# Hash-bucket attention: the bucket mask as sign bits, with its bias in the exponential's scale

## The chip, the cores and the metric

The kernel runs on one core of a Trainium2 chip. The metric is the device time of one execution in microseconds (us). The core has a matrix engine (PE, with its weight loads shown apart as PEld), a vector engine (DVE), a scalar engine for activations (ACT), a general engine (POOL), and a queue engine (SP) that issues DMAs. Each engine works through its own list in order; ACT and POOL also issue DMAs.

## What is computed

Two stages run in one kernel. The first is attention over 4 x 8 heads of 768 tokens with head size 64, where a query sees a key only if both fall into the same hash bucket. The bucket is made of six bits, each the sign of a projection:

```python
q_bits = (np.einsum('bhsd,dk->bhsk', q, proj) > 0).astype(np.int64)
k_bits = (np.einsum('bhsd,dk->bhsk', k, proj) > 0).astype(np.int64)
q_bucket = np.sum(q_bits * powers, axis=-1)      # powers of two
...
mask = q_bucket[:, :, :, None] == k_bucket[:, :, None, :]
scores = scale * np.matmul(q, k.transpose(0, 1, 3, 2))
scores = np.where(mask, scores, -1000000000.0)
...
attn = np.exp(scores)
attn = attn / (np.sum(attn, axis=-1, keepdims=True) + 1e-09)
return np.matmul(attn, v).astype(np.float32)
```

The second stage takes the 3072 x 512 result through an RMS norm and a gated feed-forward layer (`silu(xn @ w_gate) * (xn @ w_val) @ w_out`, inner size 1536).

## The kernel before

All heads are worked one after the other, i = 0 to 31, and the prologue of a head runs two heads ahead of its main part (the loop at L379 to L389). A planner orders each engine's instructions and sets the waits; the source does not write that order out.

**Prologue of a head (L136 to L249).** For q and then for k, a DMA on SP's queue loads the head (L145). PE transposes it in six blocks (L153) into PSUM, in two halves of 384 tokens. DVE copies each half to the float32 tile `tf` (L157) and casts it to bf16 into rows 0 to 63 of `tq` (L159, times the softmax scale) or `tk` (L167). PE multiplies `tf` by the projection (L171), which leaves six rows of 384 numbers in PSUM. DVE compares them with zero and writes rows 64 to 69 of the same tile: 0 or 120 for a query (L179), -0.5 or +0.5 for a key (L188). These six rows make the score matmul add a term that depends on the bits in common. Next comes a bias per key: six matmuls with one output column each (L214) multiply the key's six bit rows by -60, and DVE adds -178 (L221). With it the exponent is the score plus 2 where all bits agree, and lower by at least 60 where one differs. Last, a row for a small term of the denominator is made (L234, L243).

All PSUM tiles of the prologue (transposes, projections, biases, the small row, and the sums of the RMS norm) take turns in one pool, `pro`, that has two buffers. A third tile must wait until the first has been read.

**Main part of a head (L251 to L330).** For each of six key blocks, PE makes 128 x 768 scores (L269, 70 rows deep) in one of two score buffers, and ACT takes the exponential to fp16 with the per-key bias (L278). PE accumulates values times exponentials (L289, L298). DVE moves the result to SBUF (L308); the denominator goes to DRAM and back on POOL's queue, DVE inverts it (L317), and it returns as a broadcast (L322) for the multiplication into `xt` (L325).

**RMS norm (L332 to L377).** For each 512 tokens ACT squares (L337), PE sums (L338), ACT takes a square root (L351), and DVE inverts one row of 512 (L355) and corrects it (L357 to L364). The row goes through DRAM to a broadcast, and POOL multiplies (L375). Four of the six blocks run within the attention loop, when the last head of their batch is done.

**Weights.** ACT's queue issues 20 loads of feed-forward weights, one emitted with each of the first 20 heads (L122, L133). They use one or two staging buffers, which DVE empties by a cast (L123, L134).

**Feed-forward (L391 to L440).** Six blocks of 512 tokens: 96 matmuls for gate and value (L403, L411), a sigmoid on ACT (L419), two DVE products (L421, L424), then the output matmuls (L429).

Of the kernel before, what the change touches and what calls it, by code (L numbers as in the profile page):

```python
# [9 lines left out]
FP32 = mybir.dt.float32  # L10
BF16 = mybir.dt.bfloat16
FP16 = mybir.dt.float16

AF = mybir.ActivationFunctionType
ALU = mybir.AluOpType
# [3 lines left out]
def kernel(  # L19
# [12 lines left out]
    nc = tc.nc  # L32

    B, H, S, D = q.shape
    NB = S // 128
# [7 lines left out]
    NTS = NT // 512  # L43
    scale = 1.0 / (D ** 0.5)

    QSCL = 120.0
    KOFF = 0.5
    BETA = 2.0
    BIAS_RHS = -60.0
    BIAS_ADD = BETA - 180.0  # L50
    DELTA = 1.0e-9

    def ts_ready_head(tsi):
# [4 lines left out]
    const = ctx.enter_context(tc.tile_pool(name="const", bufs=1))  # L58
# [7 lines left out]
    nc.gpsimd.memset(proj_sb[:], 0.0)  # L66
    nc.scalar.dma_start(out=proj_sb[0:64, 0:n_bits], in_=proj[:, :])

    biascol = const.tile([128, 1], BF16, tag="c_biascol")
    nc.gpsimd.memset(biascol[:], BIAS_RHS)  # L70
    deltacol = const.tile([128, 1], FP16, tag="c_deltacol")
    nc.gpsimd.memset(deltacol[:], 1.0)
    ones_bf = const.tile([128, 512], BF16, tag="c_onesbf")
# [6 lines left out]
    for dc in range(NDC):  # L80
        nc.scalar.dma_start(
            out=rmsg_col[0:128, dc : dc + 1],
            in_=moe_rms_g[bass.ts(dc, 128)].rearrange("(p x) -> p x", x=1),
# [16 lines left out]
    bias_sb_tiles = [None] * NHEAD  # L100
# [8 lines left out]
    with (  # L109
# [26 lines left out]
        def emit_prologue(i):  # L136
            b, h = head_bh(i)
            tq = att.tile([128, S], BF16, name=f"tq{i}", tag="tqk", bufs=8)
            tk = att.tile([128, S], BF16, name=f"tk{i}", tag="tqk", bufs=8)
            tq_tiles[i] = tq  # L140
            tk_tiles[i] = tk

            for which, src, tdst in (("q", q, tq), ("k", k, tk)):
                nat = att.tile([128, NB, 64], FP32, tag="qknat", bufs=6)
                nc.sync.dma_start(  # L145
                    out=nat[:], in_=src[b, h].rearrange("(p n) d -> p n d", n=NB)
                )
                tf = att.tile([64, S], FP32, tag="tf", bufs=3)
                for half in range(2):
                    tps = pro_ps.tile([64, 3, 128], FP32, tag="pro")  # L150
                    for j in range(3):
                        sc = half * 3 + j
                        nc.tensor.transpose(  # L153
                            out=tps[:, j, :], in_=nat[:, sc, :], identity=ident[:]
                        )
                    cols = bass.ds(half * 384, 384)
                    nc.vector.tensor_copy(out=tf[0:64, cols], in_=tps[:, :, :])  # L157
                    if which == "q":
                        nc.vector.tensor_scalar(  # L159
                            out=tdst[0:64, cols],  # L160
                            in0=tf[0:64, cols],
                            scalar1=scale,
                            scalar2=None,
                            op0=ALU.mult,
                        )
                    else:
                        nc.vector.tensor_copy(out=tdst[0:64, cols], in_=tf[0:64, cols])  # L167
                for half, n in ((0, 384), (1, 384)):
                    bps = pro_ps.tile([128, n], FP32, tag="pro")
                    cols = bass.ds(half * 384, n)  # L170
                    nc.tensor.matmul(  # L171
                        out=bps[64:70, 0:n],
                        lhsT=proj_sb[0:64, 0:n_bits],
                        rhs=tf[0:64, cols],
                        start=True,
                        stop=True,
                    )
                    if which == "q":
                        nc.vector.tensor_scalar(  # L179
                            out=tdst[64:70, cols],  # L180
                            in0=bps[64:70, 0:n],
                            scalar1=0.0,
                            scalar2=QSCL,
                            op0=ALU.is_gt,
                            op1=ALU.mult,
                        )
                    else:
                        nc.vector.tensor_scalar(  # L188
                            out=tdst[64:70, cols],
                            in0=bps[64:70, 0:n],  # L190
                            scalar1=0.0,
                            scalar2=KOFF,
                            op0=ALU.is_gt,
                            op1=ALU.subtract,
                        )

            if h % 2 == 0:
                vt = att.tile([128, NB, 193], FP16, name=f"vt{i}", tag="vt", bufs=3)
                vt_tiles[i // 2] = vt
                nc.gpsimd.memset(vt[:, :, 64:66], 1.0)  # L200
                nc.gpsimd.memset(vt[:, :, 66:129], 0.0)
                for hh, col0 in ((h, 0), (h + 1, 129)):
                    vnat = att.tile([128, NB, 64], FP32, tag="vnat", bufs=2)
                    nc.sync.dma_start(
                        out=vnat[:],
                        in_=v[b, hh].rearrange("(p n) e -> p n e", n=NB),
                    )
                    nc.vector.tensor_copy(out=vt[:, :, col0 : col0 + 64], in_=vnat[:])

            bias_sb = att.tile([128, 8], FP32, name=f"bias{i}", tag="bsb", bufs=4)  # L210
            bias_sb_tiles[i] = bias_sb
            bps = pro_ps.tile([128, 8], FP32, tag="pro")
            for kc in range(NB):
                nc.tensor.matmul(  # L214
                    out=bps[0:128, kc : kc + 1],
                    lhsT=tk[64:70, bass.ts(kc, 128)],
                    rhs=biascol[64:70, 0:1],
                    start=True,
                    stop=True,
                )  # L220
            nc.vector.tensor_scalar(  # L221
                out=bias_sb[0:128, 0:NB],
                in0=bps[0:128, 0:NB],
                scalar1=BIAS_ADD,
                scalar2=None,
                op0=ALU.add,
            )

            vcols = bass.ds(0, 65) if h % 2 == 0 else bass.ds(65, 128)
            M = 65 if h % 2 == 0 else 128  # L230
            vt = vt_tiles[i // 2]
            vbps = pro_ps.tile([1, 128], FP32, tag="pro")
            for jc in range(NB):
                nc.tensor.matmul(  # L234
                    out=vbps[0:1, 0:M],
                    lhsT=deltacol[0:128, 0:1],
                    rhs=vt[:, jc, vcols],
                    start=(jc == 0),
                    stop=(jc == NB - 1),
                )  # L240
            vbrow = att.tile([1, 128], BF16, name=f"vbr{i}", tag="vbr", bufs=4)
            vbrow_tiles[i] = vbrow
            nc.vector.tensor_scalar(  # L243
                out=vbrow[0:1, 0:M],
                in0=vbps[0:1, 0:M],
                scalar1=DELTA / float(S),
                scalar2=None,
                op0=ALU.mult,
            )  # L249

        def emit_main(i):  # L251
# [1 line left out]
            even = h % 2 == 0  # L253
            tq = tq_tiles[i]
            tk = tk_tiles[i]
            bias_sb = bias_sb_tiles[i]
            vt = vt_tiles[i // 2]
            vbrow = vbrow_tiles[i]
            dci = h // 2
# [6 lines left out]
            for kc in range(NB):  # L266
                sct = sc_ps.tile([128, 1024], FP32, tag="sc")
                for qs, n in ((0, 512), (1, 256)):
                    nc.tensor.matmul(  # L269
                        out=sct[0:128, bass.ds(qs * 512, n)],  # L270
                        lhsT=tk[0:70, bass.ts(kc, 128)],
                        rhs=tq[0:70, bass.ds(qs * 512, n)],
                        start=True,
                        stop=True,
                    )
                u = att.tile([128, S], FP16, name=f"u{i}_{kc}", tag="u", bufs=6)
                u_tiles[i][kc] = u
                nc.scalar.activation(  # L278
                    out=u[:, :],
                    in_=sct[0:128, 0:S],  # L280
                    func=AF.Exp,
                    bias=bias_sb[0:128, kc : kc + 1],
                    scale=1.0,
                )

            avt = av_ps.tile([128, 1024], FP32, name=f"av{i}", tag="av")
            for jc in range(NB):
                for qs, n in ((0, 512), (1, 256)):
                    nc.tensor.matmul(  # L289
                        out=avt[0:M, bass.ds(qs * 512, n)],  # L290
                        lhsT=vt[:, jc, vcols],
                        rhs=u_tiles[i][jc][:, bass.ds(qs * 512, n)],
                        start=(jc == 0),
                        stop=False,
                    )
                u_tiles[i][jc] = None
            for qs, n in ((0, 512), (1, 256)):
                nc.tensor.matmul(  # L298
                    out=avt[0:M, bass.ds(qs * 512, n)],
                    lhsT=vbrow[0:1, 0:M],  # L300
                    rhs=ones_bf[0:1, 0:n],
                    start=False,
                    stop=True,
# [167 lines left out]
```

## Time and profile before

| quantity | value |
|---|---|
| median of 6 runs | 666.25 us (641.85 to 676.97) |
| the profiled execution: its time, and the span of its instructions | 640.58 us, 638.8 us |
| PE busy | 569.9 us (89%) |
| DVE busy | 424.0 us (66%) |
| ACT busy | 244.3 us (38%) |
| POOL busy | 110.3 us (17%) |
| mean granted PE clock | 0.909 |

The profile is of one execution. Its page gives busy time by engine, then the span in 40 slices of 16 us with the clock granted to PE in tenths of full speed, then groups of instructions by source line (count, busy time, mean length in ns, and the idle time before them with what ended it). A busy PE is not a PE at its peak, because matmuls overlap and their ends are modelled; so the distance from one start to the next tells more than a length. Rows of a timeline give start, length, engine, line, operation, and in brackets the idle time before and what ended it.

### The profile page before, as it was taken

The numbers are of one execution on the slowest core, as the hardware profiler recorded it, in microseconds if no ns is written. First come the engines' busy times: TensorE is split into PE (matmuls) and PEld (weight loads), VectorE is DVE, ScalarE is ACT, GpSimd is POOL, SyncE is SP. The second block draws the span as 40 slices with busy tenths as digits, with TensorE's granted clock in tenths as the row PEclk, the third lists the DMA queues.
The fourth block names the chain that finished last, engine by engine and source line by source line (L and its number), as shares of the span: only waits on it lengthen the run. The fifth ranks groups of instructions, "written<-read, shape, count | busy, mean of one in ns | idle before, by whom it ended". The sixth has DMA issues, their size and how long they took to land. (4 is left out here: it accounts for less than half of the span.)

```text
span 638.8 us, 7718 instructions
## 1 busy us (share of the span) xinstructions
PE 569.9 (89%) x2744; PEld 234.2 (37%) x2744; DVE 424.0 (66%) x794; ACT 244.3 (38%) x312; POOL 110.3 (17%) x196
## 2 busy tenths in 40 slices
PE   1999999979999956999997899984998999999997
PEld 0334343423443311334342233331443434444443
DVE  2668678786777768658778656532839395748473
ACT  0245454443645461445554235332333241313130
POOL 1002212223212224322131302112003020000000
PEclk9999899986999975889997769657999999999999
DMA  8536544432234331232331111001010101010101
GB/s 257 181 114 197 168 131 114 116 116 62 68 88 112 88 87 47 62 88 79 97 108 48 41 46 51 25 27 51 1 66 18 66 18 50 17 63 4 67 1 66
DMA packets 27362, 49.57 MB, mean 78 GB/s; under 512 B 6582, under 2 KB 18870, under 8 KB 27324
## 3 DMA queue, kind: packets, MB, share of 16 engines
q1 hardware_dynamic: 18156, 26.76, 13.4%
q0 software_dynamic: 5632, 12.89, 7.4%
q10 hardware_dynamic: 3536, 9.44, 4.5%
q8 instruction: 21, 0.34, 0.2%
q14 instruction: 17, 0.14, 0.1%
HBM read 42.57 MB, written 6.50 MB: 77 GB/s over the span
## 5 line engine op out<-in xcount | busy, mean ns | idle before, releaser
L171 PE MATMUL bps<-tf,proj_sb 64*6 64x384 f32 x256 | 116.9, 546 | 18.8 <-DVE tf L157 17.2
L153 PE MATMUL tps<-ident,nat 128*64 128x128 f32 x384 | 72.0, 315 | 17.3 <-DMA nat<-in_q_dram 3.7
L157 DVE COPY tf<-tps 64x384 f32<-64x384 f32 x128 | 67.9, 542 | 26.4 <-PE tps L153 25.5
L419 ACT ACTIVATE sg<-gps 128x512 f16<-128x512 f32 x72 | 42.3, 597 | 104.3 <-PE gps L403 104.2
L153 PEld LDWEIGHTS tps<-ident,nat 128*64 128x64 f32 x384 | 43.9, 126 | 44.6 <-issue 5.8
L421 DVE TENSOR_TENSOR sgv<-gps,sg 128x512 f16<-128x512 f32 x72 | 49.0, 685 | 16.0 <-ACT sg L419 15.8
L424 DVE TENSOR_TENSOR hx<-vps,sgv 128x512 f16<-128x512 f32 x72 | 49.2, 688 | 6.4 <-PE gps L403 0.5
L437 DVE COPY osb<-ops 128x512 f32<-128x512 f32 x24 | 16.6, 692 | 40.5 <-PE ops L429 40.5
L429 PEld LDWEIGHTS <-hx 128*128 128x128 f16 x288 | 28.2, 98 | 34.0
L403 PE MATMUL gps<-xn_91,wg_95 128*128 128x512 f16 x72 | 27.5, 383 | 13.2 <-DVE sgv L421 12.2
L171 PEld LDWEIGHTS bps<-tf,proj_sb 64*6 64x6 f32 x256 | 12.3, 83 | 70.7 <-DVE tf L157 43.6
L318 POOL DMA_DIRECT2D dinv_scratch<-denr x32 | 18.2, 569 | 109.4 <-DVE denr L317 77.4
L309 POOL DMA_DIRECT2D den_scratch<-avsb x32 | 17.2, 536 | 107.8 <-DVE avsb L308 67.1
L411 PE MATMUL vps<-xn_91,wv_99 128*128 128x512 f16 x72 | 27.5, 382 | 0.3 <-DVE hx L424 0.3
L411 PE MATMUL vps<-xn_94,wv_102 128*128 128x512 f16 x72 | 27.5, 382 | 0.0
L403 PE MATMUL gps<-xn_93,wg_97 128*128 128x512 f16 x72 | 27.5, 382 | 0.0
L403 PE MATMUL gps<-xn_94,wg_98 128*128 128x512 f16 x72 | 27.5, 382 | 0.0
L411 PE MATMUL vps<-xn_92,wv_100 128*128 128x512 f16 x72 | 27.5, 382 | 0.0
L411 PE MATMUL vps<-xn_93,wv_101 128*128 128x512 f16 x72 | 27.5, 382 | 0.0
L403 PE MATMUL gps<-xn_92,wg_96 128*128 128x512 f16 x72 | 27.5, 382 | 0.0
L322 POOL DMA_DIRECT2D dinvb<-dinv_scratch x32 | 17.4, 544 | 37.4 <-DMA dinv_scratch<-denr 37.2
L313 POOL DMA_DIRECT2D denr<-den_scratch x32 | 18.4, 576 | 25.0 <-DMA den_scratch<-avsb 24.1
(1008 smaller groups left out, 1058.8 us busy)
## 6 DMA issues: line engine op xcount, KB each, us to landing
dinvb<-dinv_scratch POOLq DMA_DIRECT2D x32, 384.0 KB, 3.9
nat<-in_q_dram SPq DMA_DIRECT2D x32, 192.0 KB, 2.5
nat<-in_k_dram SPq DMA_DIRECT2D x32, 192.0 KB, 2.4
vnat<-in_v_dram SPq DMA_DIRECT2D x32, 192.0 KB, 2.6
out_dram<-osb SPq DMA_DIRECT2D x24, 256.0 KB, 2.0
st<-in_moe_w_gate_dram ACTq DMA_DIRECT2D x4, 768.0 KB, 4.7
st<-in_moe_w_out_dram ACTq DMA_DIRECT2D x12, 256.0 KB, 4.8
st<-in_moe_w_val_dram ACTq DMA_DIRECT2D x4, 768.0 KB, 4.2
```

Source lines behind the costliest of these rows:

```text
L153: nc.tensor.transpose(out=tps[:, j, :], in_=nat[:, sc, :], identity=ident[:])
L157: nc.vector.tensor_copy(out=tf[0:64, cols], in_=tps[:, :, :])
L171: nc.tensor.matmul(out=bps[64:70, 0:n], lhsT=proj_sb[0:64, 0:n_bits], rhs=tf[0:64, cols], start=True, stop=True,)
L313: nc.gpsimd.dma_start(out=denr[0:128, 0:6], in_=den_dram[i].rearrange("(p x) -> p x", x=6),)
L318: nc.gpsimd.dma_start(out=dinv_dram[i].rearrange("(p x) -> p x", x=6), in_=denr[0:128, 0:6])
L322: nc.gpsimd.dma_start(out=dinvb[:, :], in_=dinv_dram[i : i + 1, :].to_broadcast((128, S)))
L403: nc.tensor.matmul(out=gps[:], lhsT=wg_sb[dc][:, bass.ts(fc, 128)], rhs=xn[dc][:, cols], start=(dc == 0), stop=(dc == NDC - 1),)
L411: nc.tensor.matmul(out=vps[:], lhsT=wv_sb[dc][:, bass.ts(fc, 128)], rhs=xn[dc][:, cols], start=(dc == 0), stop=(dc == NDC - 1),)
L419: nc.scalar.activation(out=sg[:], in_=gps[:], func=AF.Sigmoid)
L421: nc.vector.tensor_tensor(out=sgv[:], in0=gps[:], in1=sg[:], op=ALU.mult)
L424: nc.vector.tensor_tensor(out=hx[:], in0=vps[:], in1=sgv[:], op=ALU.mult)
L429: nc.tensor.matmul(out=ops[:], lhsT=ht[fc][:, bass.ts(tci, 128)], rhs=wo_sb[fc][:], start=(fc == 0), stop=(fc == NFC - 1),)
```

## The change

The six bit rows of both tiles now hold the sign of the projection, -1 or +1, written by ACT's Sign function straight from PSUM, in place of DVE's two comparisons. Their product over six rows is 6 where all bits agree and at most 4 otherwise. The exponential's scale is 30, so agreement adds 180 and one differing bit takes 60 away; a constant bias of -178 for every key leaves +2 for agreement. The query's scale is divided by 30 to match. The per-key bias, its six matmuls and its DVE addition are gone, with their PSUM tile.

```diff
-    QSCL = 120.0
-    KOFF = 0.5
+    MSC = 30.0
     BETA = 2.0
-    BIAS_RHS = -60.0
-    BIAS_ADD = BETA - 180.0
...
-    biascol = const.tile([128, 1], BF16, tag="c_biascol")
-    nc.gpsimd.memset(biascol[:], BIAS_RHS)
+    expbias = const.tile([128, 1], FP32, tag="c_expbias")
+    nc.gpsimd.memset(expbias[:], BETA - 180.0)
...
-                            scalar1=scale,
+                            scalar1=scale / MSC,
...
-                    if which == "q":
-                        nc.vector.tensor_scalar(
-                            out=tdst[64:70, cols],
-                            in0=bps[64:70, 0:n],
-                            scalar1=0.0,
-                            scalar2=QSCL,
-                            op0=ALU.is_gt,
-                            op1=ALU.mult,
-                        )
-                    else:
-                        nc.vector.tensor_scalar(
-                            out=tdst[64:70, cols],
-                            in0=bps[64:70, 0:n],
-                            scalar1=0.0,
-                            scalar2=KOFF,
-                            op0=ALU.is_gt,
-                            op1=ALU.subtract,
-                        )
+                    nc.scalar.activation(
+                        out=tdst[64:70, cols], in_=bps[64:70, 0:n], func=AF.Sign
+                    )
...
-            bias_sb = att.tile([128, 8], FP32, name=f"bias{i}", tag="bsb", bufs=4)
-            bias_sb_tiles[i] = bias_sb
-            bps = pro_ps.tile([128, 8], FP32, tag="pro")
-            for kc in range(NB):
-                nc.tensor.matmul(
-                    out=bps[0:128, kc : kc + 1],
-                    lhsT=tk[64:70, bass.ts(kc, 128)],
-                    rhs=biascol[64:70, 0:1],
-                    start=True,
-                    stop=True,
-                )
-            nc.vector.tensor_scalar(
-                out=bias_sb[0:128, 0:NB],
-                in0=bps[0:128, 0:NB],
-                scalar1=BIAS_ADD,
-                scalar2=None,
-                op0=ALU.add,
-            )
...
-                    bias=bias_sb[0:128, kc : kc + 1],
-                    scale=1.0,
+                    bias=expbias[0:128, 0:1],
+                    scale=MSC,
```

## The prediction

> **What bounds the kernel now.** I read the page's busy rows and its slices first. PE is busy for 89% of the span, DVE 66%, ACT 38%. The granted-clock row says more: it holds at 9, with dips to 5, 6 or 7 that all lie in the first 28 slices (up to 447 us), the attention part.
>
> ```profile
> PE 569.9 (89%) x2744; PEld 234.2 (37%) x2744; DVE 424.0 (66%) x794; ACT 244.3 (38%) x312; POOL 110.3 (17%) x196
> ...
> PEclk9999899986999975889997769657999999999999
> ```
>
> So next come the stage windows (columns: window, its length, busy time and instruction count of PE, PEld, DVE, ACT, POOL, then granted clock, DMA share, GB/s).
>
> ```profile
> 160.00:228.00 68.00, 64.35 (x370) 27.06 (x368) 48.36 (x109) 37.18 (x45) 14.90 (x31) 1.00 0.32 89
> ...
> 135.00:160.00 25.00, 20.20 (x84) 7.40 (x85) 19.03 (x33) 8.71 (x10) 8.39 (x11) 0.66 0.29 81
> 228.00:262.00 34.00, 22.26 (x69) 6.47 (x67) 26.83 (x40) 11.43 (x15) 15.13 (x17) 0.55 0.25 70
> 340.00:380.00 40.00, 32.55 (x121) 11.63 (x120) 26.63 (x45) 14.52 (x16) 9.35 (x13) 0.66 0.17 52
> ```
>
> ```profile
> 443.00:638.80 195.80, 185.91 (x848) 82.80 (x847) 123.89 (x178) 55.35 (x89) 9.89 (x8) 0.98 0.09 36
> ```
>
> The reader is to see three regimes. From 443 us on is the feed-forward part, PE busy 186 of 196 us; the change touches nothing there. In quiet attention (160 to 228 us) the clock is full and PE is busy 95%. Over the quiet windows 25:135, 160:228 and 262:340, 146 exponentials ran, 24.3 heads in 256 us, so 10.5 us a head. The third regime is three disturbed stretches, 99 us in all, where the RMS chains run and the clock falls to a mean of 0.55 to 0.66. There DVE is busy 67 to 79%, about as in quiet heads (71%), while PE falls to 65 to 81%.
>
> The timeline of the first of these shows the wait (start, length, instruction, and in brackets idle time before it and what ended it).
>
> ```profile
> 137.31 0.56 DVE L188 TENSOR_SCALAR tk_1297<-bps 6x384 bf16<-6x384 f32 x1 [0.51 <-PE bps L171]
> 137.90 3.34 DVE L355 RECIPROCAL r_1277<-r_1277 1x512 f32<-1x512 f32 x1
> ...
> 141.27 0.56 DVE L188 TENSOR_SCALAR tk_1297<-bps 6x384 bf16<-6x384 f32 x1
> ...
> 141.88 0.23 PE L214 MATMUL bps<-biascol,tk_1297 6*128 6x1 bf16 x3 [2.57 <-DVE tk_1297 L188]
> ```
>
> The key threshold's second half stands behind the 3.34 us reciprocal on DVE, the bias matmul behind the threshold, and PE idles 2.57 us.
>
> **The change part by part.** Built, the changed program has 384 fewer PE rows, 160 fewer DVE rows, 128 more on ACT, the same number on POOL and SP, and the same 12 activation table loads. Nothing is added to a DMA queue.
>
> *Bias matmuls removed (192 matmuls, 192 weight loads).* In a head they come in two groups of three:
>
> ```profile
> 309.75 0.22 PE L214 MATMUL bps<-biascol,tk_2970 6*128 6x1 bf16 x3
> 309.90 0.50 PE L234 MATMUL vbps<-vt_2887,deltacol 128*1 128x128 f16 x6
> ```
>
> From one start to the next is 0.15 us for three, so 0.31 us a head at most; where a group lies between the two L298 matmuls (308.66 to 308.90) it is nearly free, so 0.16 at least. Over 32 heads that is 5 to 10 us; I take 8. It lies on PE, which sets the pace.
>
> *DVE work removed.* 128 thresholds (L179, L188) at 0.555 us are 71 us, and 32 bias additions (L221) at 0.165 are 5 us: 76 of 424. DVE is not the bound, so only waits of PE on DVE count. In 160:228 the weight load of the bit projection (L171) waited for the copy L157 11 times, 3.7 us in all; with 7 heads there that is 0.53 us a head. A head has 6.9 us of DVE work (48.36 by 7) and loses 2.4 of it (4 x 0.555 + 0.165), so I take half of the wait, 0.27 us, and 26 undisturbed heads (158 exponentials): 7 us, bounds 0 and 14.
>
> *Waits in the RMS stretches.* PE waited 2.57 us (at 141.88), 2.61 (244.60, for a query threshold), 1.95 (348.35, for a bias addition behind the reciprocal) and 2.78 us (366.62, for a key threshold behind two slow casts), 9.9 us in sum. These operations leave DVE. What is late next: the copies L157 and the casts still queue behind the reciprocal, and the score matmuls of the second half need the cast. So 0 to 10; I take 8.
>
> *Clock.* By finer windows the granted clock is 0.50 from about 138.5 to 155 (first RMS chain), in the last attention chain from about 343 to 360, and again from 367 to 377. PE was busy for some 11, 13 and 9 us of these at half speed; at full speed half of that, 16.5 us, is won. The Trainium skill ("TensorE: Matmul & The Clock Gate", Part 1: The HAM clock gate) says the clock halves after an idle window of about 3.4 us and returns after about 3.4 us of work. The rows differ: it fell with PE idle for less than 2.6 us at a time, and took 9 us of dense work from 146 on to return. By the page a 2.6 us gap would cost nothing beyond itself, and this term is 0; by the trace it is up to 16.5. Each drop began amid several small waits, of which the change removes some, so I take a third, 5.5.
>
> *Signs added on ACT (128).* No row has this form. The nearest rows are
>
> ```profile
> L419 ACT ACTIVATE sg<-gps 128x512 f16<-128x512 f32 x72 | 42.3, 597 | 104.3 <-PE gps L403 104.2
> ...
> L278 ACT ACTIVATE u_2_353<-sct,bias_183 128x768 f16<-128x768 f32 x1 | 0.9, 902 | 3.4 <-PE sct L269 3.4
> ```
>
> Both read PSUM. The slope between them is 1.19 ns an element, so 384 elements take 0.45 us (slope) to 0.60 (no slope); I take 0.5, which makes 64 us in all. The skill speaks against such a move ("ScalarE: Activation LUTs", Rules for kernel authors): simple elementwise operations belong on VectorE, up to about three times faster there. By that rule a Sign would be 3 x 0.555 = 1.67 us; with six exponentials at 0.80 us spacing (4.8) ACT would need 11.5 us a head, more than the 10.5, and the kernel would lose some 30 us. By the rows ACT needs 4.8 + 2.0 = 6.8 us and has room. The rows decide.
>
> The cost of a Sign is then its place. ACT works in order. A Sign waits behind exponentials, and the exponential after it waits for the bit projection on PE. It frees one of the two "pro" buffers, for which PE's next transpose or projection waits. In the built order the Signs stand in ones and twos among the exponentials, and PE's order puts score and output matmuls between a projection and the next user of its buffer (rows of 0.33 us each), so most of the delay is covered; uncovered it is up to an exponential, 0.9 us. I take 0.05 us each, 6 us; bounds 0 and 0.45 us (58 us). A gain from buffers freed earlier is not counted here, since DVE's own delays are in the terms above. ACT's queue also carries 20 weight loads, some of which wait for a DVE cast of an earlier stage; Signs now stand behind them, but in the first heads the exponentials already did (the first started at 24.75 us), so nothing is added.
>
> *Edits with no cost of their own:* the other scalar in L159, the constant bias column and scale 30 in the exponential. An exponential also no longer waits for a bias addition (2.5 to 3.4 us of ACT's idle per head), which is not on PE's path in quiet heads.
>
> **Sum.** -8 - 7 - 8 - 5.5 + 6 = -22.5 us. Against the profiled execution, 640.58 us, that is 618. The median of the six runs shown is 666.25, 26 above the profiled run, and the runs spread over 35 us. I suppose that the spread is half-clock time, which one trace cannot show; I carry the saving over unscaled: 666.25 - 22.5 = 644 us.
>
> **The rivals.**
> - *More than forecast: the clock holds.* All 16.5 us of half-clock loss go (11 more), the whole 14 us of copy waits (7 more), the stalls fully (2 more): 624 us. For it: DVE loses 18% of its work. Against: the double RMS chain (228 to 262) has two reciprocals in a row and no prologue work ahead in either order.
> - *Given back: the pace is held elsewhere.* PE's gaps move from DVE to ACT, and only the low end of the bias matmuls is won: 661 us. For it: a busy 95% hides how long PE truly works, and the copy waits are small beside it.
> - *Slower: Signs stuck behind exponentials.* If each of the 128 Signs frees its buffer half an exponential (0.45 us) later than PE can cover, it costs 58 us against 28.5 won: +29, so 695 us. It breaks even at 0.22 us a Sign and is slower by over 2% from 0.32. For it: two buffers only, and an in-order engine with 0.9 us instructions. Against: ACT idles half of a quiet head (37 of 68 us busy).
> - *It doesn't do what it says:* Sign forcing table loads of 1.28 us around it. The built program has 12 loads before and after, so this has no chance.
>
> **How the numbers follow.** Forecast 0.45, clock holds 0.20, given back 0.18, slower 0.17. A measurement of this kernel can tell about 2% (13 us) from no change. Faster by over 2% (under 653): 0.62, the first two less 0.03 for a forecast that falls short. Within 2%: 0.21. Slower: 0.17. For 8 in 10 I leave out 0.07 below 614 and 0.12 above 680. The forecast's own range is 630 to 655.
>
> **What would show it.** Right: quiet heads at about 9.8 to 10.2 us; no PE wait on a threshold beside the reciprocal; a shorter third regime with a mean clock above 0.66 in the first and third stretch; Sign rows near 0.5 us; DVE busy near 348 us, ACT near 308. Wrong: waits of transposes or projections on ACT by a Sign that sum to over 28 us; Sign rows above 1 us; quiet heads at 10.5 us or more; or a clock that falls as long as before for another reason.

## The result, and the profile after

The changed kernel takes 639.88 us (median of 10 runs, 635.92 to 656.0) against 662.39 us for the kernel before, run beside it (20 runs, 641.85 to 682.77). The ratio is 0.9879, with a 95% interval of 0.983 to 0.9928: 1.2% faster, some 8 us (5 to 11) of 662, where the forecast had 22.5 us. The ratios compare undisturbed runs only, while medians count all runs; in the table below two single runs, of 2834 and 1032 us, are left out.

The median alone lies near the forecast of 644, and the two medians are even 22.5 us apart. That is luck: over 57 runs of the kernel before and 30 of the changed one the medians are 14 us apart (658.0 and 644.4), and 11 us of that are time lost to a lower clock (table below), for which the forecast had 5.5. The sum in the prediction was made against an execution of 640.58 us and gave 618. A like execution of the changed kernel took 636.90 us (span 635.1), 19 us more than that. It is the one read here. Its busy row and its clock row:

```profile
PE 565.1 (89%) x2552; PEld 230.0 (36%) x2552; DVE 357.4 (56%) x634; ACT 306.3 (48%) x440; POOL 112.7 (18%) x196
...
PEclk9998898897979985559999886996999999999999
```

DVE fell from 424 to 357 us and ACT rose from 244 to 306, as forecast (348 and 308). PE is as busy as before, 89%, and the dips of the clock are still there: the mean granted clock is 0.909 in both executions. By stages (window, length, busy time and count of PE, PEld, DVE, ACT, POOL, granted clock, DMA share, GB/s):

```profile
184.00:228.00 44.00, 42.69 (x222) 17.89 (x221) 23.38 (x52) 31.49 (x45) 9.66 (x20) 0.98 0.30 86
228.00:290.00 62.00, 48.00 (x147) 15.42 (x145) 32.88 (x48) 27.70 (x39) 18.39 (x22) 0.59 0.21 60
286.10:350.00 63.90, 61.94 (x321) 25.15 (x320) 33.69 (x80) 43.17 (x63) 13.70 (x27) 0.98 0.32 91
350.00:395.00 45.00, 40.00 (x166) 15.34 (x165) 28.06 (x45) 28.40 (x38) 13.46 (x21) 0.77 0.22 60
443.00:635.10 192.10, 184.72 (x846) 82.36 (x844) 122.09 (x176) 51.73 (x84) 9.90 (x8) 0.99 0.10 36
```

The three regimes remain. In quiet attention PE is busy 97%, DVE now only 53%. The disturbed stretch around the double RMS chain (228 to 290) has a clock of 0.59 and PE at 77%. The feed-forward part is what it was.

For the pace of a head at full clock I took the starts of all 192 exponentials from the trace, and from 55 us on the mean distance between neighbours with no half-clock record in between, times six. That is 10.31 us a head before, and 9.67, 9.72 and 10.23 in three executions of the changed kernel. One list of instructions thus gives values up to 0.56 us apart. The gain, 0.1 to 0.6 us a head, holds that of the removed bias matmuls (0.16 to 0.31 in the prediction), but this measure cannot tell whether there is more.

### The profile page after: what moved, and what is told of

It is laid out like the page before. It is cut to its first block, busy times and chain, and to the rows that moved or that the text cites. A ratio compares the mean times of both kernels' runs of the same rounds, so it can differ in the third digit from the quotient of the medians.

```text
span 656.9 us, 7286 instructions
## 1 busy us (share of the span) xinstructions
PE 589.2 (90%) x2552; PEld 236.6 (36%) x2552; DVE 354.4 (54%) x634; ACT 307.0 (47%) x440; POOL 112.6 (17%) x196
## 5 line engine op out<-in xcount | busy, mean ns | idle before, releaser
L168 PE MATMUL bps<-tf,proj_sb 64*6 64x384 f32 x256 | 126.6, 585 | 23.6 <-DVE tf L154 22.5
L150 PE MATMUL tps<-ident,nat 128*64 128x128 f32 x384 | 76.5, 329 | 12.7 <-DMA nat<-in_q_dram 3.7
L150 PEld LDWEIGHTS tps<-ident,nat 128*64 128x64 f32 x384 | 45.7, 131 | 46.9 <-issue 8.6
L383 DVE TENSOR_TENSOR sgv<-gps,sg 128x512 f16<-128x512 f32 x72 | 49.0, 685 | 16.8 <-ACT sg L381 16.7
L365 PE MATMUL gps<-xn_91,wg_95 128*128 128x512 f16 x72 | 27.8, 385 | 13.5 <-DVE sgv L383 12.5
L271 POOL DMA_DIRECT2D den_scratch<-avsb x32 | 16.8, 525 | 118.5 <-DVE avsb L270 83.8
L275 POOL DMA_DIRECT2D denr<-den_scratch x32 | 19.8, 617 | 49.4 <-DMA den_scratch<-avsb 49.1
L284 POOL DMA_DIRECT2D dinvb<-dinv_scratch x32 | 17.7, 554 | 36.7 <-DMA dinv_scratch<-denr 35.5
```

The costliest lines, as they stand in the source:

```text
L150: nc.tensor.transpose(out=tps[:, j, :], in_=nat[:, sc, :], identity=ident[:])
L168: nc.tensor.matmul(out=bps[64:70, 0:n], lhsT=proj_sb[0:64, 0:n_bits], rhs=tf[0:64, cols], start=True, stop=True,)
L275: nc.gpsimd.dma_start(out=denr[0:128, 0:6], in_=den_dram[i].rearrange("(p x) -> p x", x=6),)
L284: nc.gpsimd.dma_start(out=dinvb[:, :], in_=dinv_dram[i : i + 1, :].to_broadcast((128, S)))
L365: nc.tensor.matmul(out=gps[:], lhsT=wg_sb[dc][:, bass.ts(fc, 128)], rhs=xn[dc][:, cols], start=(dc == 0), stop=(dc == NDC - 1),)
L383: nc.vector.tensor_tensor(out=sgv[:], in0=gps[:], in1=sg[:], op=ALU.mult)
```

## Where the rest went: waits that change places

A Sign has the length that was forecast (0.5 us). These are the groups of ACT in the changed kernel (count, busy time, mean ns of one, then idle time just before and what ended it):

```profile
L240 ACT ACTIVATE u<-sct,expbias 128x768 f16<-128x768 f32 x192 | 165.7, 900 | 31.7 <-PE sct L231 27.2 <-DMA st<-in_moe_w_out_dram 1.6
...
L175 ACT ACTIVATE tq<-bps 6x384 bf16<-6x384 f32 x64 | 30.8, 481 | 66.0 <-PE bps L168 65.5
L175 ACT ACTIVATE tk<-bps 6x384 bf16<-6x384 f32 x64 | 30.8, 481 | 53.6 <-PE bps L168 52.9
```

What was not foreseen is the right-hand side: ACT stood 118 us at Signs whose projection was not there yet. Before the change ACT's idle time stood in front of exponentials, mostly those whose scores or bias were not there yet. In front of a Sign it holds up the exponential behind it. A place where this is plain, from the timeline (start, length, and in brackets idle time before and what ended it):

```profile
54.47 0.28 PE L231 MATMUL sct<-tq,tk 70*128 70x256 bf16 x1
...
55.17 1.30 DVE L190 CAST vt<-vnat 128x384 f16<-128x384 f32 x2 [0.22 <-issue]
56.39 0.94 DVE L270 COPY avsb<-av 128x768 f32<-128x768 f32 x1
57.26 1.00 DVE L154 COPY tf<-tps 64x384 f32<-64x384 f32 x2
...
57.85 1.45 PE L168 MATMUL bps<-tf,proj_sb 64*6 64x384 f32 x4 [1.24 <-DVE tf L154]
...
58.69 0.48 ACT L175 ACTIVATE tq<-bps 6x384 bf16<-6x384 f32 x1 [4.06 <-PE bps L168]
59.20 0.90 ACT L240 ACTIVATE u<-sct,expbias 128x768 f16<-128x768 f32 x1
```

The scores of that exponential were ready at 54.75. It started at 59.20, because a Sign of a later head was ahead of it in ACT's list. That Sign waited for a projection, the projection for a copy, and the copy stood on DVE behind two casts of values and a copy of the output.

I added up, over all 192 exponentials, the time from the (modelled) end of their second score matmul to their start: 85 us before, 166 after, and in 81 of the 192 cases a Sign lay in between. With the comparisons on DVE (the experiment below) the sum is 67 us.

How much of this reaches PE is another question. These are the groups of score matmuls, first in the changed kernel, then with the comparisons on DVE; the last number is PE's idle time before them that an exponential ended:

```profile
L231 PE MATMUL sct<-tq,tk 70*128 70x512 bf16 (+1 forms) x384 | 107.7, 361 | 9.4 <-ACT u L240 8.2
...
L236 PE MATMUL sct<-tq,tk 70*128 70x512 bf16 (+1 forms) x384 | 106.6, 359 | 10.9 <-ACT u L245 9.0
```

PE waited 8.2 us for late exponentials with the Signs, and 9.0 without them (6.6 in the kernel before). For the Signs themselves its matmuls waited 1.8 us in sum, and its weight loads, which overlap the matmuls, 17 us; the prediction had set 28 us of such waits as a sign of being wrong. So the delays on ACT are real, but the waits of PE do not show that they cost time.

The first heads show a delay too. The prediction held that nothing would be added there; but two Signs of the next head stand ahead of the first exponential:

```profile
21.66 0.48 ACT L175 ACTIVATE tk<-bps 6x384 bf16<-6x384 f32 x1 [0.80 <-PE bps L168]
...
26.12 0.48 ACT L175 ACTIVATE tq<-bps 6x384 bf16<-6x384 f32 x1 [3.98 <-PE bps L168]
27.40 0.48 ACT L175 ACTIVATE tq<-bps 6x384 bf16<-6x384 f32 x1 [0.80 <-PE bps L168]
27.91 2.69 ACT L240 ACTIVATE u<-sct,expbias 128x768 f16<-128x768 f32 x3
```

The first exponential starts at 27.91 us, against 24.75 before, 3.2 us later. This is a matter of the planned order more than of the Signs: in the experiment that keeps the bias work these two Signs lie behind the first exponentials, and the first one starts at 23.39.

On DVE, the work that left did not shorten PE's waits. First the views of the waits between 25 and 443 us in the kernel before (engine, line, what it waited for: sum in us, times, longest), then in the changed kernel:

```profile
PE bps L171 <- DVE tf L157: 6.6, 7, 1.8
...
PEld bps L171 <- DVE tf L157: 30.1, 60, 3.1
...
DVE tf L157 <- PE tps L153: 25.3, 34, 2.0
```

```profile
PE bps L168 <- DVE tf L154: 12.7, 11, 2.9
...
PE tps L150 <- DVE vbr L206: 6.3, 4, 2.6
...
PEld bps L168 <- DVE tf L154: 25.4, 36, 3.4
...
DVE tf L154 <- PE tps L150: 73.8, 56, 4.0
```

The projections' waits for the copies are 36.7 us before and 38.1 after. DVE's relief shows as DVE waiting for the transposes, 73.8 us in place of 25.3.

I also added up all waits of PE over 0.15 us, from 25 us to the last exponential. Those that DVE ended are 24.8 us before and 17.5 to 21.5 in three executions of the changed kernel; those that ACT ended are 10.0 before and 15.9 to 16.8 after. Together that is 34.8 before and 34.3 to 37.4 after: what DVE no longer holds up, ACT does.

Of the waits of PE that are longer than 1 us in attention, the sum is 19.2 us (10 of them) before and 24.6 us (13) after (20.3 and 23.2 in the other two executions). The thresholds beside the reciprocal are gone from that list, as forecast; in their place stand the small row `vbr` and the copy `tf`, which were next in DVE's list. One of the new ones begins with a late broadcast:

```profile
89.94 0.95 DVE L287 TENSOR_TENSOR xt<-avsb,dinvb 64x768 f32<-64x768 f32 x1 [4.13 <-DMA dinvb<-dinv_scratch]
90.82 0.61 DVE L164 CAST tk<-tf 64x384 bf16<-64x384 f32 x2
91.35 0.21 DVE L206 TENSOR_SCALAR vbr<-vbps 1x65 bf16<-1x65 f32 x1
...
91.62 0.30 PE L150 MATMUL tps<-ident,nat 128*64 128x128 f32 x1 [2.65 <-DVE vbr L206]
...
92.34 0.90 ACT L240 ACTIVATE u<-sct,expbias 128x768 f16<-128x768 f32 x1 [2.65 <-PE sct L231]
```

DVE reached the multiplication into `xt` before its broadcast had landed and stood there for 4.13 us, with two casts and the small row queued behind it; PE then waited 2.65 us for the row's buffer, and ACT for PE. All such stands of DVE at the broadcast sum to 23.8 us between 25 and 443 us, against 16.4 before (9.1, 4.0, 1.8 and 1.5 by output tile).

Two others, of 2.87 us (up to 178.68) and 2.54 us (up to 383.40), stand behind a DVE operation that takes 0.35 us elsewhere and here 4.6 or 4.7, while POOL multiplies:

```profile
172.39 4.90 DVE L156 TENSOR_SCALAR tq<-tf 64x384 bf16<-64x384 f32 x2
171.87 4.94 POOL L337 TENSOR_TENSOR xn<-xt,rb 128x512 f16<-128x512 f32 x4
...
378.54 4.67 DVE L164 CAST tk<-tf 64x384 bf16<-64x384 f32 x1
378.06 4.92 POOL L337 TENSOR_TENSOR xn<-xt,rb 128x512 f16<-128x512 f32 x4
```

The clock fell right after both, at 178.93 and 383.73. The kernel before has the like (4.04 us at 361.93, the slow cast ahead of the prediction's wait at 366.62), so the move of the bits does not reach the root of these waits.

## The experiments

Three theories were on record. A: the Signs' place in ACT's queue gives back what DVE's relief wins. B: the Signs cost nothing and the relief counts. C: PE's own work and its clock set the time, whatever DVE and ACT do. The table has all experiments. Medians count all runs of the kernel; the ratios are against the kernel before in the same call; "lost to the clock" is the mean of span x (1 - granted clock), an estimate of what the lower clock cost, as if PE had worked throughout; "the rest" is the mean span without it.

| kernel | runs | median, us | ratio [95%] in each call | lost to the clock, us | the rest, us |
|---|---|---|---|---|---|
| before, in all later calls | 57 | 658.0 | | 81 | 579 |
| after | 30 | 644.4 | 0.9826 [0.9638, 1.0015]; 0.9929 [0.9811, 1.0046] | 70 | 573 |
| bias folded, bits compared on DVE | 17 | 633.1 | 0.9826 [0.9708, 0.9943]; 0.9761 [0.9581, 0.9941]; 0.9672 [0.9445, 0.9899] | 54 | 578 |
| Signs on ACT, bias work kept | 12 | 649.2 | 0.9934 [0.9827, 1.0042] | 68 | 581 |
| query bits on ACT, key bits on DVE | 12 | 641.1 | 0.9867 [0.9779, 0.9955] | 69 | 571 |
| short Signs | 6 | 635.1 | | 60 | 574 |
| each Sign twice | 6 | 674.9 | 1.044 [1.0289, 1.059] | 85 | 590 |
| each comparison twice | 6 | 720.3 | 1.1155 [1.0997, 1.1313] | 126 | 594 |
| no bits | 12 | 655.6 | 1.0106 [1.0007, 1.0205] | 70 | 587 |

One caution holds for all of them. The planner makes a new order for each kernel, and PE's matmuls come in another order in every one of these; an edit is therefore never tested alone.

**The changed kernel again.**

> The changed kernel as it is, again, for a second profile and as the mark for the runs beside it. Both theories: 0.983 to 0.993 of the kernel before. The profile: half-clock stretches at other places than in the first one; span less half of the half-clock time about 572 to 578 us, against 581 us for the kernel before (638.8 less half of 116).

> The changed kernel again, beside the variant with the bits compared on DVE, on the same chip. Theory A (the Signs give back what DVE's relief wins, and only the folded bias counts): within 1% of that variant, either way. Theory B (DVE's relief is worth something and the Signs nothing): 10 us or more faster than that variant.

It took 639.35 us (6 runs, 631.33 to 653.57) and 648.16 us (12 runs, 636.63 to 654.05). In neither call does the interval of the ratio exclude 1, so the gain is small here too. The profile's span less half of its half-clock time is 577 us, as expected. Over all 30 runs of this kernel the median is 644.4, 14 us under that of the kernel before.

**The bias folded away, the bits left on DVE.** Half of the change alone, run three times:

```diff
-    MSC = 30.0
+    MSC = 120.0
...
-                    nc.scalar.activation(
-                        out=tdst[64:70, cols], in_=bps[64:70, 0:n], func=AF.Sign
-                    )
+                    nc.vector.tensor_scalar(
+                        out=tdst[64:70, cols],
+                        in0=bps[64:70, 0:n],
+                        scalar1=0.0,
+                        scalar2=0.5,
+                        op0=ALU.is_gt,
+                        op1=ALU.subtract,
+                    )
```

> The bias is folded into the scale, but the six bit rows are written by DVE as before (compare with zero, minus one half, for queries and keys alike; the exponential's scale is 120). So the 192 matmuls and 32 additions go, and nothing moves to ACT. Theory A (the Signs on ACT give back most of what DVE's relief wins, by their place in the queue): as fast as the changed kernel or faster, 0.975 to 0.99 of the kernel before. Theory B (the Signs cost nothing by their place, the relief of DVE is won, the bias matmuls are worth less than 8 us): slower than the changed kernel, 0.99 to 1.0 of before.

> The kernel with the bias folded and the bit rows on DVE, again, on the chip of these runs: 0.975 to 0.99 of the kernel before, as fast as the changed kernel within 1%.

> Bias folded away, bits by DVE's comparison, third time, beside the changed kernel. Theory A: within 1% of the changed kernel, and some 10 to 20 us faster than the kernel before. Theory B: 10 us or more slower than the changed kernel.

It took 634.87, 633.89 and 632.0 us. Beside it the changed kernel took 639.35 in the first call and 648.16 in the third: 4 and 16 us more by the medians, nothing (0.9826 for both) and 17 us by the ratios, whose intervals overlap. Theory B expected this kernel to be the slower one by 10 us or more, and falls. Theory A expected the two within 1% in the third call; they are 2.5% apart, so A has not the whole story either. This kernel is faster than the kernel before in all three calls (the three ratios average 0.975), and never slower than the changed one. Its page has DVE where it was before the change:

```profile
PE 560.3 (89%) x2552; PEld 230.9 (37%) x2552; DVE 423.1 (67%) x762; ACT 243.1 (39%) x312; POOL 111.4 (18%) x196
...
L245 ACT ACTIVATE u<-sct,expbias 128x768 f16<-128x768 f32 x192 | 164.9, 899 | 195.7 <-PE sct L236 186.9
```

ACT waits 187 us for scores and for nothing else of weight: an exponential mostly starts when its scores are ready. But PE's waits are hardly shorter: over 1 us they sum to 14.5 us (8 of them) here and to 20.0 in another execution, against 20.3 to 24.6 in the changed kernel, and over 0.15 us those ended by DVE or ACT are 32.6 and 38.0 us, against 34.3 to 37.4. A head at full clock takes 9.61 and 10.03 us, within what the changed kernel takes.

The table shows where the difference lies: outside the loss to the clock this kernel takes 5 us more than the changed one, and it loses 16 us less to the clock. Likewise, all that it wins over the kernel before is clock (54 for 81; the rest is 578 and 579). Why the clock falls less in this order of matmuls is not shown.

**The bits on ACT, the bias work left.** The other half alone; the six matmuls and DVE's addition of each head stay, with a column of zeros:

```diff
+    biascol = const.tile([128, 1], BF16, tag="c_biascol")
+    nc.gpsimd.memset(biascol[:], 0.0)
...
+            bps = pro_ps.tile([128, 8], FP32, tag="pro")
+            for kc in range(NB):
+                nc.tensor.matmul(
+                    out=bps[0:128, kc : kc + 1],
+                    lhsT=tk[64:70, bass.ts(kc, 128)],
+                    rhs=biascol[64:70, 0:1],
...
+            nc.vector.tensor_scalar(
+                out=bias_sb[0:128, 0:NB],
...
+                scalar1=BETA - 180.0,
...
-                    bias=expbias[0:128, 0:1],
+                    bias=bias_sb[0:128, kc : kc + 1],
```

> The Signs stand on ACT as in the changed kernel, and the six bias matmuls and the DVE addition per head are kept (with a zero column, so that the bias is the same constant). Theory A: little or nothing is won by moving the bit rows alone, 0.995 to 1.015 of the kernel before. Theory B: the move alone wins, 0.985 to 0.995.

It took 649.17 us, 10 us more than the changed kernel in the same call. The ratio to the kernel before, 0.9934, lies in the range that theory B gave and just outside that of A; its interval covers both and has 1 in it, so it decides nothing between them. A head at full clock takes 10.27 us, and took 10.31 before: moving the bits shortens no head that this can see. The bias work is worth about 7 us by the ratios (0.9934 less 0.9826, of 657) and 10 by the medians. Moving the bits did not raise the loss to the clock here (68 for 78 in this call), so that loss is no fixed price of a Sign.

**Each Sign twice.**

```diff
+                    nc.scalar.activation(
+                        out=tdst[64:70, cols], in_=bps[64:70, 0:n], func=AF.Sign
+                    )
```

> The changed kernel with each Sign issued twice in a row, 128 instructions more on ACT at about 0.48 us (61 us of ACT time). Theory A (each Sign delays a buffer that PE waits for): 10 to 40 us slower than the changed kernel. Theory B (covered by PE's other work): within 4 us of it.

It took 674.93 us, 35.6 us more than the changed kernel in the same call: 0.28 us for each of 128 added Signs of 0.48 us. That is more than half of their length, on an engine that is busy for half of the time, and in the range of theory A (10 to 40 us). Half of it is lost to the clock (85 for 67 in this call).

**Short Signs.** Each Sign writes 16 columns in place of 384; the other bit rows are set once, so most of the mask is left out:

```diff
+    tqk = [xtp.tile([128, S], BF16, name=f"tqk{j}", tag=f"tqk{j}") for j in range(8)]
+    for t in tqk:
+        nc.gpsimd.memset(t[64:70, :], 1.0)
...
-            tq = att.tile([128, S], BF16, name=f"tq{i}", tag="tqk", bufs=8)
-            tk = att.tile([128, S], BF16, name=f"tk{i}", tag="tqk", bufs=8)
+            tq = tqk[(2 * i) % 8]
+            tk = tqk[(2 * i + 1) % 8]
...
-                        out=tdst[64:70, cols], in_=bps[64:70, 0:n], func=AF.Sign
+                        out=tdst[64:70, bass.ds(half * 384, 16)], in_=bps[64:70, 0:16], func=AF.Sign
```

> Bias folded away, 128 Signs kept on ACT in their places, but each writes only 16 columns instead of 384 (the rest of the bit rows is preset to one once, so most of the mask is left out); the 70-row score matmuls and the order in which PE mixes prologue and main work stay close to the changed kernel's. If the Signs' time in ACT's queue gives the gain back (theory A: 0.23 us each at the margin), cutting some 0.3 us from each takes 15 to 25 us off the changed kernel: 615 to 625 us. If a Sign costs by its presence and its waits, not its length (theory A2), or if PE's own work and clock are the bound (theory C), it stays within 5 us of the changed kernel: 635 to 645.

It took 635.11 us, 13 us less than the changed kernel in the same call. The group of its Signs:

```profile
L179 ACT ACTIVATE tqk<-bps 6x16 bf16<-6x16 f32 x128 | 22.2, 175 | 112.0 <-PE bps L172 107.2 <-DMA st<-in_moe_w_out_dram 3.0
```

A Sign is 0.306 us shorter, and 0.10 us of that reaches the end: a third. The time lies at the edge of what C expected (635 to 645), but further below the changed kernel than the 5 us that C allowed; the difference is just short of what A expected (15 to 25). ACT stands at the Signs nearly as long as before, but less follows from it: 48 exponentials have a Sign between their scores and their start, not 81, and the time from scores to start is 103 us, not 166. PE's waits over 1 us sum to 12.0 us. That fits a price of the Signs that grows with their length; but all 13 us are again loss to the clock (60 for 73 in this call), and PE waits 10.3 us for exponentials here, not less than the 8.2 above, so the path from the Signs to the time is not shown.

**Half of the bits on each engine.**

```diff
-    MSC = 30.0
+    MSC = 60.0
...
-                    nc.scalar.activation(
-                        out=tdst[64:70, cols], in_=bps[64:70, 0:n], func=AF.Sign
-                    )
+                    if which == "q":
+                        nc.scalar.activation(
+                            out=tdst[64:70, cols], in_=bps[64:70, 0:n], func=AF.Sign
+                        )
+                    else:
+                        nc.vector.tensor_scalar(
+                            out=tdst[64:70, cols],
+                            in0=bps[64:70, 0:n],
+                            scalar1=0.0,
+                            scalar2=0.5,
+                            op0=ALU.is_gt,
+                            op1=ALU.subtract,
+                        )
```

> The bias folded, the query's bit rows by Sign on ACT and the key's by a comparison on DVE (minus one half; the scale is 60). Theory A: the price is in the wait of PE for the buffer, whichever engine empties it, so a split wins only what is left of queueing: 0 to 8 us faster than either whole version. A theory in which one of the queues is full predicts 8 to 20 us.

It took 641.11 us; beside it the version with all bits on DVE took 633.89. Both theories had expected the split to be the faster one. Half of the Signs cost as much as all of them, within what these runs can tell.

**Each comparison on DVE twice.** The version with the bits on DVE, with every comparison issued twice:

> The kernel with the bias folded and the bit rows on DVE, with each comparison issued twice, 128 DVE instructions more of 0.56 us (71 us). Theory A (a bit-row operation costs about the same in either queue, as the second Sign did, 0.2 to 0.3 us each): 20 to 40 us slower than the kernel with one comparison each. Theory C, and also the view that DVE had room while ACT had not: under 10 us slower.

It took 720.33 us, 86 us more than with one comparison in the same call: 0.67 us for each added operation of 0.555 us. That is far more than theory A expected (20 to 40 us), and C expected under 10. The loss to the clock rose from 56 to 126 us, so 70 of the 86 us are lost there. DVE is thus no engine with room: to add to it costs more than twice what it costs to add to ACT (0.28 us), though to take the same work off it (the move to ACT) won nothing.

**No bits at all.** Signs left out, the score matmuls 64 rows deep, so that the mask is left out of what is computed:

```diff
-                    nc.scalar.activation(
-                        out=tdst[64:70, cols], in_=bps[64:70, 0:n], func=AF.Sign
-                    )
...
-                        lhsT=tk[0:70, bass.ts(kc, 128)],
-                        rhs=tq[0:70, bass.ds(qs * 512, n)],
+                        lhsT=tk[0:64, bass.ts(kc, 128)],
+                        rhs=tq[0:64, bass.ds(qs * 512, n)],
```

> The changed kernel with the Signs left out and nothing in their place: the projections run on PE and nobody reads them, the score matmuls use the 64 data rows alone (the mask is left out). So DVE has its relief and ACT bears nothing. Theory A (the Signs by their place give back what the relief of DVE wins): 20 to 35 us faster than the changed kernel, at most 0.965 of the kernel before. Theory C (neither the bits on DVE nor the Signs on ACT are on the path; PE's own work and its clock are): within 8 us of the changed kernel.

It took 655.59 us: no faster than the kernel before, though neither ACT nor DVE makes bits. That contradicts what A and C both expected, and it is not a clean test. With the consumer of the projections gone, the planner orders PE's list otherwise: the prologue's matmuls lie in 172 groups, where the changed kernel has 207 and the version with bits on DVE 226, so they are less spread between scores and outputs. Outside the loss to the clock it takes 14 us more than the changed kernel (587 for 573), though it has less to do; this suggests that the order of PE's list can cost as much as all that this case is about. What DVE's relief would be worth without the Signs stays unmeasured.

## Why the forecast was too large

The direction was right, and the chance for faster by over 2% was too high. The step that failed is the price of moving the bits from DVE to ACT: PE's waits were to shrink by 15 us, and the Signs to cost 6. Measured, PE's waits did not shrink (34.8 us before, 34.3 to 37.4 after), and the Signs cost more. By the terms of the prediction:

- *Bias matmuls removed, -8.* Right: with the Signs in place the bias work is worth 7 to 10 us (649.2 to 639.4). By the ratios this is all that the change wins. Without the Signs its removal gives 2.5% (mean of three ratios), some 16 us, and by the table that is loss to the clock, not PE's own work.
- *DVE work removed, -7 ("half of the wait").* Not won. PE's waits for the copies are 38.1 us after 36.7. The 60 waits of the weight load before the change have a mean of 0.50 us, and the copy itself takes 0.54; so on average they may be no more than the copy's own length, which taking work off the queue does not shorten. That is argued from the sizes.
- *Waits in the RMS stretches, -8.* The threshold waits went, and others took their place. The prediction saw what is late next, the copies and casts behind the reciprocal, and still took 8 of 10. The long waits of PE came to 20.3 to 24.6 us after 19.2.
- *Clock, -5.5.* Nothing in the two profiles: their half-clock records sum to 117 us in both. Over all runs of both kernels the loss is smaller after, 70 us for 81, twice the term; that is why the medians differ by more than the ratio says. One reading in the term was wrong: it says that PE was idle for less than 2.6 us at a time where the clock fell, but the drop at 367 us came right behind the wait of 2.78 us that the prediction lists itself.
- *Signs on ACT, +6 ("0.05 us each").* Too small. The length was right; the place was not. The prediction argued that ACT "idles half of a quiet head". That idle time was spent waiting for scores or a bias, in a list that is worked in order. The Signs are in this list ahead of exponentials whose scores are ready, and wait for projections of a later head. PE's waits that ACT ended rose from 10.0 to 15.9 us or more. By experiment a Sign costs several times 0.05 us: a second one costs 0.28 us, and 0.10 us is won where a Sign is 0.306 us shorter; carried over to the whole 0.48 us that is 0.16 us each, an estimate of 20 us for 128.
- *"So nothing is added" in the first heads.* Wrong by 3.2 us in this planned order: the first exponential starts at 27.91 us.

Together: the forecast for moving the bits was -7 - 8 - 5.5 + 6 = -14.5 us (with the bias addition's small share). Measured, with the bias folded, the move costs nothing to 4 us in one call and 16 or 17 in another. It takes back part of what folding the bias wins, and some 8 us are left. The rival "given back" (661, on the median's basis) had the mechanism right as far as PE's waits go: they move from DVE (24.8 to 21.5 us or less) to ACT (10.0 to 15.9 or more). The rule that the prediction weighed and set aside, elementwise work to VectorE ("ScalarE: Activation LUTs", Rules for kernel authors), gave the better kernel here, though not for its reason: one Sign takes 0.48 us on ACT and one comparison 0.554 on DVE. The page states its factor of three for bf16; the operand here is f32 in PSUM.

What stays open: why the kernel with the bits on DVE is faster than the changed one at all. PE's waits do not show it, and the 16 us lie in the loss to the clock, while the rest is 5 us longer. That the Signs' delays bring the clock down is one reading; that this planned order of PE's list does so, whatever the Signs cost, is another, nearer to theory C. No run here separates them: a kernel with the Signs and the order of the other was not tried. What DVE's stands at the broadcast of the denominators (23.8 us) cost was not tried either.

## What to carry to other kernels

Idle time of an engine that works in order is not room: ask what an added operation waits for, and what stands behind it in the list while it waits. Here 62 us of Signs fitted into ACT's idle time by the sum, and still 81 of 192 exponentials had one in front of them; 128 more Signs cost 36 us. When a change has two parts that touch different engines, price them apart; here the part with the matmuls alone was the better kernel (633 us). And split each time into the loss to the clock and the rest before a cause is named: several of the differences here lie wholly in the first.

## What the hardware showed that was not expected

The granted clock is 1 or 0.50 in these traces, and it changes in steps of 3.413 us. Two traces differ: in that of the kernel with no bits (716.64 us) the upper level is 0.85, and one of 1032 us has no record of the clock. Once down, it can stay down under a busy PE:

```profile
91.70:105.20 13.50, 11.92 (x64) 4.91 (x65) 7.68 (x17) 7.90 (x11) 2.66 (x5) 1.00 0.47 133
...
260.00:286.00 26.00, 25.26 (x76) 8.42 (x75) 11.54 (x21) 10.87 (x17) 11.17 (x11) 0.50 0.19 48
```

From 260 to 286 us PE was busy 97% and the clock stayed at 0.50 throughout. Right after the wait of 2.65 us that ended at 91.62 it stayed at 1.00 for 13.5 us with PE busy 88%. "TensorE: Matmul & The Clock Gate" (Part 1: The HAM clock gate) gives the step, a window of 3413 ns, and says that one busy window of about 3.4 us releases the clock; the row from 260 to 286 us speaks against the second statement. PE's busy time counts matmuls that are slow because of the clock, so it may overstate the activity; what the gate counts no run here shows.

Most of the spread between runs of one kernel is this loss: over all runs of a kernel, time and loss to the clock correlate with 0.78 (before) and 0.86 (after); only with the bits on DVE is it less, 0.48.
